# Attention and SiLU layers in one hand-ordered program: the last pair stored in whole rows, loads put behind other transposes, batches 2 to 4 in another order

## The chip, the core and the metric

The kernel runs on one core of one Trainium2 chip. The metric is the device time of one execution, in microseconds (us); three executions of the kernel before were timed, and a fourth was profiled.

## The reference

The computation is a Nyströmformer attention (8 batches, 8 heads, 576 tokens, head size 64, 32 landmarks), followed by two dense layers with a SiLU between them. Cut to what matters:

```
q_lm, k_lm = q, k as means over 18 neighbouring tokens        # 32 landmarks
A  = softmax(q  @ k_lm.T / 8)      # 576 x 32
Bm = softmax(q_lm @ k_lm.T / 8)    # 32 x 32
C  = softmax(q_lm @ k.T / 8)       # 32 x 576
Z  = Bm.T / (norm1 * norminf);  6 times: Z = 2 Z - Z @ Bm @ Z
x  = A @ Z @ C @ v                 # heads side by side: 4608 x 512
h  = x @ w_in;  out = (h * sigmoid(h)) @ w_out    # 512 -> 2048 -> 512
```

## The kernel before

The program is one long list of named steps, the string `SEQUENCE`. Each step emits its instructions on one engine, and each engine runs its own instructions in the order of the list. Nothing re-orders them on the chip: an engine waits for the first instruction in its queue, however much could be done behind it. A word is `name.batch` or `name@priority`; `/ACT`, `/DVE` or `/SP` picks the engine of a step that may run on several; `x<y` adds a wait of DMA x for the landing of DMA y; `*3` stands for three small matmuls that only fill time on TensorE.

The steps of batch b, by their names:

- `ld100.b` to `ld111.b`, `ld000.b` to `ld011.b`, `ldv0.b` to `ldv2.b` load k, q and v. They are issued by GpSimd (lines 401 and 418), which queues them in the order of the list. `ld1.b`, `ld0.b` do this for batch 2.
- `xt11.b`, `xt10.b`, `xt01.b`, `xt00.b` (line 551, batches 3 to 7) are DMA transposes of k and q, `ct0.b` and `ct1.b` (line 825, batches 2 to 7) DMA transposes of exp(C). `os...` are the stores of the output (line 988). SyncE issues all of these in the order of the list; only stores of the last pairs may also be issued by ScalarE.
- `lra`, `lrb`, `lrc`, `lrd` with `1.b` or `0.b` add up landmarks on VectorE, out of what `xt1..` and `xt0..` bring. `ltr`, `lmT`, `sb`, `pb`, `pbs`, `bmx`, `csb`, `f0` and others make Bm; `ns..`, `nsd..`, `fb..` are the six iterations for Z.
- `A.b`, `C.b` are the scores, `Ax..`, `Cx..` their exponentials on ScalarE, `etn..` the normalized A. `cv.b` multiplies exp(C) with v: it reads `ct0.b`, `ct1.b` and all of v. `wc.b`, `zbd.b`, `zt.b`, `ztc.b` make Z @ C @ v, and `m0.b` to `m3.b` multiply that with w_in; `mc..` are the copies of their results on VectorE or ScalarE.
- `h0.b` to `h15.b` finish the first layer, `g..` are its SiLUs on ScalarE (`hx`, `gx`: the last 64 columns of four batches in one tile).

The second layer works on pairs of 128-token tiles with seven products instead of eight (Strassen's scheme; `layer2_pair`). A pair has a number: `5000 + 100 b + 20 p` for batch b, half p, and 5340 or 5740 for the `gx` tile of four batches. `ss..` are its operand sums on VectorE, `p1` to `p7` its products on TensorE, 8 matmuls of 256 columns each. `c1`, `u2`, `c5`, `c21` copy results to the output tiles, `c11`, `c12`, `c22` add to them on VectorE. A pair has two output tiles: the low one is complete after `c11` (left half of its columns) and `c12` (right half), the high one after `c22` and `c21`. A store `os0` to `os3` sends 32 rows of 512 columns. `os@5100.0` is the low tile of pair 5100, in four stores, `os@5101.0` its high tile.

All TensorE steps share eight PSUM banks, and `SEQUENCE` decides which bank a step gets. The order of the DMAs is set by SyncE's and GpSimd's queues and by the `<` waits, which keep the transposes and the loads of one stage apart.

Of the kernel before, what the change touches and what calls it, by code (L numbers as in the profile page):

```python
# [42 lines left out]
trc15.2/DVE h14.0 g14.0 ns50.1 nsd50.1 zbd.1 ldv2.1 cv0.1 wc.1 tr114.2 trc114.2/DVE tr19.2
trc19.2/DVE zt.1 g8.0 ztc.1/ACT tr10.2 trc10.2/DVE lra1.2 h7.0 g7.0 m3.1 mc31.1/ACT mc30.1/ACT
m1.1 mc11.1/DVE mc10.1/ACT h1.0 g1.0 ld0.2 tr00.2 lrb1.2 tr09.2 tr014.2 trc014.2/DVE tr05.2
trc05.2/DVE trc09.2/DVE lrc1.2 trc00.2/ACT h12.1 g12.1 h7.1 g7.1 h15.1 m2.1 mc20.1/ACT m0.1
mc00.1/ACT mc21.1/ACT mc01.1/ACT wo0 o0@5001.0 h14.1 g14.1 g15.1 o0@5000.0 fold lrd1.2 lra0.2
lrb0.2 lrc0.2 lrd0.2 h11.1 g11.1 ltr0.2 ltr1.2 lmT1.2/DVE lmT0.2/ACT ss00@5020.0 ss10@5020.0
ss20@5020.0 ss30@5020.0 wo1 h5.1 o1@5000.0 sb.2 pb.2 pbs.2 pbr.2 bmx.2 bmt.2 wo2 wt00 bbd.2 h8.1
h3.1 o1@5001.0 o2@5000.0 wo3 o2@5001.0 wt01 g8.1 csb.2 o3@5001.0 oc@5001.0/ACT g3.1 g5.1 n1.2  # L50
nrm.2 stz.2 o3@5000.0 hx8.1 f0.2 gx8.1 h0.1 g0.1 oc@5000.0/ACT h2.1 h10.1 g10.1 h4.1 h1.1 g2.1
g1.1 wt11 wt21 stf0.2 fb00.2 ns00.2 h13.1 g13.1 wt31 nsd00.2 fb10.2 wt10 wt20 wt30 p1@5020.0
c1@5020.0/ACT ns10.2 nsd10.2 fb20.2 h9.1 h6.1 g4.1 g9.1 g6.1 ss00@5100.0 p5@5020.0 c5@5020.0/DVE
hx0.1 gx0.1 ss10@5100.0 l1done.0 C.2 Cx00.2 Cx10.2 p6@5020.0 u2@5020.0/DVE ld100.3 ld101.3 ld110.3
# [24 lines left out]
ld010.5 ld011.5 ss10@5200.0 lra1.4 lrb1.4 lrc1.4 ss10@5220.0 ss20@5220.0 lrd1.4 lra0.4 lrb0.4
os@5020.0 ss20@5200.0 l1done.2 ltr1.4 h1.3 h0.3 g0.3 g1.3 g12.3 h15.3 gx0.3 c1@5200.0/DVE  # L80
p6@5200.0 u2@5200.0/ACT os@5021.0 ss30@5200.0 c5@5200.0/DVE p3@5200.0 ss30@5220.0 lmT1.4/DVE
lrc0.4 lrd0.4 ltr0.4 lmT0.4/ACT g15.3 p1@5220.0 sb.4 pb.4 c1@5220.0/ACT xt11.5<ldv1.5
xt10.5<ldv1.5 c12@5200.0 p7@5200.0 c22@5200.0 p2@5200.0 c11@5200.0 p4@5200.0 c21@5200.0/ACT
p6@5220.0 xt01.5<ldv1.5 pbs.4 u2@5220.0/ACT pbr.4 l1done.3 bmx.4 bmt.4 bbd.4 ss00@5300.0
xt00.5<ldv1.5 C.4 lra1.5 csb.4 os@5120.0 Cx10.4 os@5121.0 Cx00.4 f0.4 p5@5220.0 Cx11.4 p7@5220.0
n1.4 lrb1.5 lrc1.5 os@5200.0 Cx01.4 nrm.4 ct0.4<ldv1.5 lrd1.5 c5@5220.0/ACT stf0.4 A.4 Ax00.4
Ax01.4 p5@5300.0 ltr1.5 fb00.4 Ax10.4 p3@5220.0 S10.4 Ln10.4 Ax11.4 wrc.4 stz.4 p1@5300.0 ns00.4
ss10@5300.0 ss20@5300.0 ss30@5300.0 c1@5300.0/ACT S00.4 S11.4 c22@5220.0 lra0.5 p4@5220.0 Ln11.4
Rs1.4 p6@5300.0 nsd00.4 lrb0.5 lrc0.5 lrd0.5 S01.4 fb10.4 lmT1.5/DVE ld000.6<xt00.5 ltr0.5
# [13 lines left out]
ct1.5<ldv1.6 u2@5340.0/ACT g5.4 g7.4 fb40.5 ns40.5 nsd40.5 fb50.5 p7@5340.0 ss30@5340.0 ns50.5
nsd50.5 c22@5340.0 h14.4 h12.4 g4.4 zbd.5 m0.4 g9.4 ldv2.5<xt00.4 g12.4 mc00.4/ACT mc01.4/DVE
cv0.5 wc.5 h11.4 h1.4 g11.4 g14.4 c11@5340.0 xt00.6<ldv1.6 zt.5 p3@5340.0 ztc.5/DVE etn0.5 g1.4
ldv0.7<xt00.6 c12@5340.0 ldv1.7<xt00.6 m0.5 ldv2.7<xt00.6 ld100.7<xt00.6 ld101.7 mc01.5/ACT m3.5
mc00.5/ACT ld110.7 ld111.7 m1.5 ldv2.6<xt00.5 mc10.5/ACT xt10.6<ldv1.6 l1done.6 xt11.6<ldv1.6
ldv0.6<xt00.5 ld000.7<xt00.6 mc11.5/DVE h0.4 h10.4 mc30.5/DVE h13.4 ld001.7 g10.4 g13.4 h4.5
# [1064 lines left out]
```

## Time and profile before

| | us |
|---|---|
| Median of three executions (240.06 to 241.44) | 240.55 |
| The profiled execution | 240.4 |
| Its span, first to last instruction | 238.7 |
| TensorE busy in the span | 230.6 |
| VectorE busy | 182.8 |
| ScalarE busy | 182.6 |
| GpSimd busy | 49.4 |

The profiled execution took 1.7 us more than its span. All instants in this text count from the span's start. The granted TensorE clock is 0.997 over the span. TensorE's matmuls overlap in the records, so that "busy" doesn't mean "at its peak"; what a step costs TensorE is the distance from its start to the start of the next one. Likewise the cost of an instruction in a queue of VectorE or ScalarE is the distance between two starts, a little under the duration in the record.

### The profile page before, as it was taken

The numbers are of one execution on the slowest core, as the hardware profiler recorded it, in microseconds if no ns is written. First come the engines' busy times: TensorE is split into PE (matmuls) and PEld (weight loads), VectorE is DVE, ScalarE is ACT, GpSimd is POOL, SyncE is SP. The second block draws the span as 40 slices with busy tenths as digits, with TensorE's granted clock in tenths as the row PEclk, the third lists the DMA queues.
The fourth block names the chain that finished last, engine by engine and source line by source line (L and its number), as shares of the span: only waits on it lengthen the run. The fifth ranks groups of instructions, "written<-read, shape, count | busy, mean of one in ns | idle before, by whom it ended". The sixth has DMA issues, their size and how long they took to land.

```text
span 238.7 us, 7507 instructions
## 1 busy us (share of the span) xinstructions
PE 230.6 (97%) x2948; PEld 163.7 (69%) x2948; DVE 182.8 (77%) x507; ACT 182.6 (76%) x434; POOL 49.4 (21%) x89
## 2 busy tenths in 40 slices
PE   6999999999999989999999999999999999999991
PEld 4887556456876745687878655768876645799881
DVE  2689889898998669939999789858998665538751
ACT  3599999989889988996867998999779797803100
POOL 0836652240055008103060074000000000000000
PEclk9999999999999999999999999999999999999998
DMA  6999999999999997998979999995527540012355
GB/s 251 265 202 186 202 212 205 208 205 180 160 162 190 231 229 137 202 155 174 196 132 202 174 163 243 220 173 119 104 54 112 122 102 1 3 44 48 89 124 142
DMA packets 56163, 37.72 MB, mean 158 GB/s; under 512 B 37056, under 2 KB 47552, under 8 KB 56128
## 3 DMA queue, kind: packets, MB, share of 16 engines
q0 software_dynamic: 15168, 17.18, 44.9%
q1 hardware_dynamic: 40144, 19.12, 39.0%
...
q8 instruction: 23, 0.38, 0.7%
...
## 4 chain that ended last, share of the span: by engine, by line
PE 90%; ACT 3%; DMA 3%; issue 1%; SPq 1%; DVE 0%; DVEq 0%
PE ps L337 87%; DMA gm<-in_q_dram 3%; PE ps L527 2%; ACT gm L923 1%; PE ps L813 1%; ACT L1126 1%; SPq L382 1%; ACT gx L946 0%; ACT pb L652 0%; ACT qk L347 0%; ACT et L753 0%; DVE wsb L856 0%; DVE ost L349 0%; ACT ost L347 0%; DVEq L856 0%
## 5 line engine op out<-in xcount | busy, mean ns | idle before, releaser
L923 ACT ACTIVATE gm<-ps 128x512 f16<-128x512 f32 x128 | 68.2, 626 | 4.9 <-PE ps L337 4.6
L337 PE MATMUL ps<-etn,m 128*128 128x64 bf16 (+1 forms) x512 | 70.9, 286 | 0.0
L337 PEld LDWEIGHTS <-gm 128*128 128x128 f16 x512 | 48.8, 98 | 11.0 <-issue 1.0
L337 PE MATMUL ps<-w_out_sb,gm 128*128 128x256 f16 (+1 forms) x392 | 52.5, 281 | 0.0
L337 PEld LDWEIGHTS <-m 128*128 128x128 bf16 x512 | 31.4, 98 | 23.0 <-issue 2.6
L337 PEld LDWEIGHTS <-ss 128*128 128x128 f16 x408 | 38.4, 98 | 7.8 <-issue 1.8
L337 PE MATMUL ps<-wt,ss 128*128 128x256 f16 x272 | 35.0, 273 | 0.0
L347 ACT COPY ost<-ps 128x256 f32<-128x256 f32 (+1 forms) x46 | 17.7, 392 | 18.8 <-PE ps L337 11.9
L1046 DVE TENSOR_TENSOR ost<-ost,ps 128x256 f32<-128x256 f32 x51 | 20.7, 415 | 10.7 <-PE ps L337 7.2
L349 DVE CAST m<-ps 128x512 bf16<-128x512 f32 x29 | 18.8, 685 | 3.6 <-PE ps L337 3.5
L418 POOL DMA_DIRECT2D v<-in_v_dram x24 | 14.5, 619 | 29.6 <-PE ps L337 27.3
L347 ACT CAST m<-ps 128x512 bf16<-128x512 f32 x35 | 18.9, 608 | 2.1 <-PE ps L337 2.1
L721 DVE SCALAR_TENSOR_TENSOR st<-st,ps 128x128 bf16<-128x128 bf16 (+2 forms) x54 | 13.6, 257 | 7.9 <-PE ps L337 7.1
L337 PE MATMUL ps<-w_out_sb,ss 128*128 128x256 f16 x136 | 17.6, 273 | 0.0
L401 POOL DMA_DIRECT2D qk<-in_k_dram x20 | 10.5, 546 | 34.1 <-DMA qT<-qk 15.8
L349 DVE COPY ost<-ps 128x256 f32<-128x256 f32 x24 | 10.1, 420 | 7.5 <-PE ps L337 7.1
L337 PE MATMUL ps<-wt,gm 128*128 128x256 f16 x120 | 15.5, 273 | 0.0
L946 ACT ACTIVATE gx<-ps 128x512 f16<-128x512 f32 x16 | 9.8, 619 | 7.5 <-PE ps L337 7.4
L696 DVE TENSOR_TENSOR fb<-st,hmask 128x256 bf16<-128x256 bf16 (+1 forms) x54 | 14.5, 273 | 1.1
L401 POOL DMA_DIRECT2D qk<-in_q_dram x20 | 10.5, 543 | 22.2 <-issue 14.0
L798 ACT ACTIVATE ce<-ps 128x288 bf16<-128x288 f32 x32 | 12.9, 417 | 2.3 <-PE ps L337 2.3
L763 ACT ACTIVATE ln<-ps 128x288 f32<-128x288 f32 x32 | 12.3, 428 | 3.0 <-PE ps L337 2.8
...
## 6 DMA issues: line engine op xcount, KB each, us to landing
out_dram<-ost SPq DMA_DIRECT2D x128, 64.0 KB, 2.9
...
```

Of the source, the lines that this page charges most:

```text
L337: nc.tensor.matmul(out=out_ap, lhsT=lhsT, rhs=rhs, start=start, stop=stop, skip_group_check=True)
L347: nc.scalar.copy(out=out, in_=in_)
L349: nc.vector.tensor_copy(out=out, in_=in_)
L401: lambda e, t=t, g=g, h=h, src=src: nc.gpsimd.dma_start(out=qk_r[b % 2][64 * h:64 * h + 64, t, g].rearrange("p j d -> p (j d)"), in_=src[b ...
L418: lambda e, a=a: nc.gpsimd.dma_start(out=v_r[b % 2][a * L:(a + 1) * L, :, :], in_=v[b].rearrange("h (l a x) d -> a l h (x d)", l=L, a=VA)[ ...
L696: nc.vector.tensor_tensor(out=fb[it % 2][:, g0:g1], in0=bc(sr[it % 3][:, g0:g1, 0:L], 4, 2), in1=bc(hmask, n, 1), op=OP.mult), [o], 14.5 + ...
L721: nc.vector.scalar_tensor_tensor(out=s2[:, g0:g1, lo:SW], in0=s[:, g0:g1, lo:SW], scalar=2.0, in1=ps[:, 0:NG * SW].rearrange("p (g x) -> p ...
L763: lambda e, g=g, c=c, ln=ln: nc.scalar.activation(out=ln[:, c], in_=bank(me["S", g, c])[:, 0:HS], func=AF.Ln),
L798: nc.scalar.activation(out=ce[:, :, 0:VP].rearrange("p (i c) (a l) -> p c a i l", c=2, a=VA)[:, c], in_=bank(me["C"], 2 * g + c)[:, 0:HS]. ...
L923: lambda e, dc=dc, cell=cell: nc.scalar.activation(out=gm[:, dc, :], in_=bank(cell["o"]), func=AF.Silu),
L946: lambda e, d0=d0, cell=cell, c=c: nc.scalar.activation(out=gx[:, d0:d0 + 8, c:c + 64], in_=bank(cell["o"]).rearrange("p (c x) -> p c x", ...
L1046: nc.vector.tensor_tensor(out=out_, in0=x, in1=y, op=OP.add)
```

## The change

There are three parts.

**Stores of the last pair.** The pair 5740 ends the kernel. Its low tile was stored in eight half rows (`os00` to `os03` after `c11`, `os10` to `os13` after `c12`, each 32 rows of 256 columns); it is now stored in four whole rows after both. The stores of the last four half-pairs were handed to SyncE and ScalarE one by one; they now stand directly behind the add that releases them, in turns by the two queues. The copy `c21@5720` moves from ScalarE to VectorE.

**Loads of batches 4 to 6.** `ld100.4` waited for `xt00.3` and now waits for `ct0.2`. In batch 6, the three v loads and four k loads are re-ordered: `ldv0.5` and `ldv2.5` lead and wait for `ct1.4`; `ldv1.6`, which comes last, keeps its wait for `xt00.5`. `ct0.5` and `ct1.5` no longer wait for `ldv1.6`.

**Order.** The steps from the end of batch 1's attention to the middle of batch 4's are listed in another order (from about 26 us to 142 us of the span), and some copies change between ScalarE and VectorE. No arithmetic is added or dropped; both lists hold 64 filler matmuls and the ScalarE program holds 12 table loads in each. GpSimd's queue keeps its order but for the two loads named; SyncE's queue keeps its order but for the last stores.

The diff, cut to what the text speaks of:

```diff
-mc10.0/DVE m0.0 f0.1 mc01.0/DVE mc00.0/ACT *1 ctm10.1 ctc10.1/DVE Rs1.1 csb.1 *1 h4.0 n1.1 m3.0
...
-ct0.2<ldv1.3 os@5000.0 ld100.4<xt00.3 ld101.4 ld110.4 ld111.4 lra1.3 fb30.2 ns30.2 p2@5020.0
...
-zbd.2 zt.2 ztc.2/ACT S10.3 Ln10.3 p4@5100.0 Cx11.3 ss00@5120.0 c11@5100.0 os@5100.0 ss10@5120.0
-ss20@5120.0 p1@5120.0 S01.3 Ln01.3 m3.2 mc31.2/ACT bmx.3 wrc.3 mc30.2/DVE c21@5100.0/ACT os@5101.0
-ct1.3<ldv1.4 m2.2 mc21.2/DVE mc20.2/ACT bmt.3 p5@5120.0 S00.3 m0.2 m1.2 mc11.2/DVE csb.3 bbd.3
...
-ns50.3 nsd50.3 zbd.3 h11.2 g11.2 h13.2 h3.2 cv0.3 wc.3 g4.2 g13.2 g3.2 etn1.3 zt.3 ztc.3/DVE
-etn0.3 p3@5120.0 c12@5120.0 m3.3 mc30.3/ACT m0.3 mc01.3/DVE mc00.3/ACT m2.3 mc21.3/ACT m1.3
...
-p2@5220.0 u2@5300.0/ACT p7@5300.0 ss00@5320.0 Ln01.4 c12@5220.0 lmT0.5/DVE sb.5 c21@5220.0/ACT
...
-c5@5300.0/ACT p3@5300.0 c12@5300.0 c22@5300.0 C.5 Cx01.5 cv0.4 wc.4 ldv1.6<xt00.5 bmt.5 Cx11.5
...
+mc10.0/DVE m0.0 mc01.0/DVE mc00.0/ACT *1 Rs1.1 csb.1 n1.1 nrm.1 ld1.2 ldv2.1 *1 h5.0 m3.0 ld0.2
...
+nsd10.1 h9.0 h10.0 fb20.1 ns20.1 g12.0 h8.0 g9.0 hx8.0 nsd20.1 fb30.1 g10.0 gx8.0 ctm10.1 etn0.1
...
+fb50.2 ld100.4<ct0.2 ld101.4 lmT0.3/ACT ld110.4 c12@5100.0 ld111.4 Rs1.2 A.3 os@5001.0 cv0.2
...
+m0.2 m1.2 mc01.2/ACT c11@5100.0 mc11.2/DVE p6@5120.0 f0.3 csb.3 n1.3 nrm.3 stf0.3 mc10.2/DVE
+fb00.3 p2@5120.0 c11@5120.0 h12.2 os@5100.0 os@5101.0 c5@5120.0/ACT u2@5120.0/ACT ct1.3<ldv1.4
...
+etn0.3 g2.2 c21@5120.0/ACT cv0.3 ld100.5<xt10.4 nsd50.3 ld101.5 wc.3 g9.2 zbd.3 p3@5120.0 zt.3
...
+mc10.3/ACT ldv0.4 m3.3 mc31.3/DVE h6.2 h2.3 lra1.4 h3.3 h4.3 mc30.3/ACT g6.2 h1.3 h7.3 g2.3 lrb1.4
...
+ss30@5220.0 xt00.5<ldv1.5 ss30@5300.0 C.4 Cx00.4 os@5120.0 lra1.5 p4@5200.0 p6@5220.0 pb.4 pbs.4
...
+fb20.4 C.5 pbr.5 ld101.6 ld110.6 c1@5320.0/DVE cv0.4 wc.4 bmx.5 ld111.6 ldv1.6<xt00.5 Cx01.5
+os@5201.0 p7@5300.0 ns20.4 c11@5320.0 p6@5320.0 nsd20.4 fb30.4 bmt.5 c22@5300.0 Cx11.5 os@5221.0
...
+os0@5720.0/ACT os2@5720.0/SP os3@5720.0/ACT p5@5740.0 c21@5720.0/DVE os0@5721.0/SP os1@5721.0/ACT
+os3@5721.0/SP os2@5721.0/ACT p7@5740.0 c5@5740.0/DVE p3@5740.0 c22@5740.0 c12@5740.0 os0@5740.0/SP
+os1@5740.0/ACT os3@5740.0/SP os2@5740.0/ACT p4@5740.0 c21@5740.0/DVE os0@5741.0/SP os1@5741.0/ACT
+os2@5741.0/SP os3@5741.0/ACT l1done.4

         for i, t, h, dep in ((lo_i, lo_t, 0, [c11, c12]), (hi_i, hi_t, 1, [c21, c22])):
-            if spread == 2 and not h:
-                ost_st[i] = [A(f"os{u}{m}@{prio + h}", [("SP", 0.46), ("ACT", 0.46)],
-                               lambda e, m=m, t=t, u=u, h=h: store(e, t, places[h], m, slice(
-                                   HM * u, HM * u + HM)), [dep[u]], prio + 0.1 * u,
-                               dma=0.1, lag=1.5) for u in range(2) for m in range(4)]
-            elif spread:
+            if spread:
                 ost_st[i] = [A(f"os{m}@{prio + h}", [("SP", 0.66), ("ACT", 0.5)],
                                lambda e, m=m, t=t, h=h: store(e, t, places[h], m), dep, prio,
                                dma=0.16, lag=3.0) for m in range(4)]
...
-                5000.0 + 100 * b + 40, 1, 2 * (b == B - 1))
+                5000.0 + 100 * b + 40, 1, int(b == B - 1))
```

More of the change, by code (lines that the diff above doesn't have):

```diff
@@ L43 @@
[L43 to L54, printed above, removed]
@@ L79 @@
[L79 to L89, printed above, removed]
-p2@5220.0 u2@5300.0/ACT p7@5300.0 ss00@5320.0 Ln01.4 c12@5220.0 lmT0.5/DVE sb.5 c21@5220.0/ACT
@@ L103 @@
[L103 to L108, printed above, removed]
@@ L115 @@
-c5@5400.0/DVE pb.6 u2@5400.0/DVE A.6 Ax00.6 Ax11.6 p3@5400.0 h3.5 Ax01.6 pbs.6 pbr.6 bmx.6 csb.6
-p1@5420.0 Ax10.6 h13.5 n1.6 g13.5 os@5321.0 c1@5420.0/DVE h10.5 nrm.6 g10.5 p7@5400.0 h9.5
-c12@5400.0 stz.6 bmt.6 bbd.6 S01.6 g3.5 S10.6 c22@5400.0 g1.5 f0.6 stf0.6 fb00.6 h6.5 h0.5 ns00.6
-p6@5420.0 g9.5 xt00.7<ldv1.7 nsd00.6 fb10.6 ns10.6 g0.5 g6.5 u2@5420.0/ACT S00.6 nsd10.6 p5@5420.0
-fb20.6 Ln10.6 ns20.6 p7@5420.0 c5@5420.0/ACT ss00@5500.0 xt10.7<ldv1.7 ss20@5500.0 S11.6 nsd20.6
-Ln01.6 ss10@5500.0 Ln11.6 xt01.7<ldv1.7 xt11.7<ldv1.7 fb30.6 os@5341.0 p4@5400.0 Ln00.6 Rs0.6
@@ L121 @@
-c22@5420.0 c21@5400.0/ACT lra1.7 lrb1.7 lrc1.7 lrd1.7 lra0.7 lrb0.7 lrc0.7 os@5340.0 lrd0.7 C.6
-Cx00.6 Cx11.6 Cx01.6 Cx10.6 wrc.6 p1@5500.0 Rs1.6 c1@5500.0/ACT p3@5420.0 c12@5420.0 p2@5500.0
-p2@5420.0 ltr1.7 ns30.6 lmT1.7/ACT c11@5500.0 ct1.6<ldv1.7 ltr0.7 p4@5420.0 lmT0.7/ACT sb.7
-p6@5500.0 nsd30.6 fb40.6 c11@5420.0 pb.7 c21@5420.0/ACT etn0.6 ss00@5520.0 ns40.6 etn1.6 A.7 pbs.7
-u2@5500.0/ACT Ax01.7 Ax10.7 p5@5500.0 p7@5500.0 Ax00.7 S10.7 S01.7 c5@5500.0/ACT S00.7
-ct0.6<ldv1.7 nsd40.6 Ln10.7 p2@5400.0 ss30@5500.0 fb50.6 ns50.6 pbr.7 bmx.7 Ln00.7 bmt.7 Ln01.7
@@ L127 @@
-csb.7 nsd50.6 n1.7 zbd.6 os@5401.0 Ax11.7 bbd.7 c11@5400.0 cv0.6 wc.6 c22@5500.0 C.7 nrm.7
-p3@5500.0 Cx01.7 zt.6 f0.7 Cx11.7 ztc.6/ACT Cx10.7 ss20@5520.0 stf0.7 p4@5500.0 Cx00.7 c12@5500.0
-S11.7 Ln11.7 ss10@5520.0 m1.6 os@5400.0 m0.6 m2.6 mc20.6/ACT mc21.6/ACT mc11.6/ACT mc10.6/DVE
-mc00.6/DVE p1@5520.0 wrc.7 stz.7 fb00.7 p2@5520.0 ns00.7 mc01.6/ACT nsd00.7 p5@5520.0 fb10.7
-c1@5520.0/ACT ns10.7 Rs0.7 ct0.7 c11@5520.0 p6@5520.0 c5@5520.0/ACT nsd10.7 fb20.7 ns20.7
-c21@5500.0/DVE h0.6 h5.6 h7.6 nsd20.7 h10.6 Rs1.7 g5.6 h3.6 ct1.7 etn1.7 fb30.7 ns30.7 g7.6
@@ new lines @@
+Ax00.3 wc.2 nsd50.2 Ax11.3 S01.3 ld010.4 ld011.4 pbs.3 c22@5100.0 Ax10.3 C.3 zbd.2 S00.3 p4@5100.0
+pbr.3 bmx.3 bmt.3 Ln01.3 zt.2 Cx11.3 S11.3 Cx01.3 Cx00.3 p1@5120.0 Ln11.3 ss00@5120.0 ss20@5120.0
+ztc.2/ACT ldv0.3 c21@5100.0/DVE ss10@5120.0 ldv2.3 Cx10.3 c1@5120.0/DVE Ln00.3 ldv2.4<xt00.3 m2.2
+mc21.2/DVE mc20.2/ACT m3.2 bbd.3 l1done.1 S10.3 Ln10.3 mc31.2/ACT mc30.2/DVE wrc.3 Rs0.3 p5@5120.0
+m0.2 m1.2 mc01.2/ACT c11@5100.0 mc11.2/DVE p6@5120.0 f0.3 csb.3 n1.3 nrm.3 stf0.3 mc10.2/DVE
+fb00.3 p2@5120.0 c11@5120.0 h12.2 os@5100.0 os@5101.0 c5@5120.0/ACT u2@5120.0/ACT ct1.3<ldv1.4
@@ new lines @@
+Ln00.5 l1done.7 ct0.5 ztc.4/ACT c1@5340.0/ACT c21@5320.0/ACT Rs0.5 ss10@5340.0 m3.4 mc30.4/ACT
+m1.4 mc31.4/DVE m2.4 mc21.4/ACT p6@5340.0 mc11.4/DVE ns20.5 mc20.4/ACT p2@5340.0 nsd20.5
+mc10.4/ACT h5.4 fb30.5 ns30.5 c5@5340.0/DVE nsd30.5 h7.4 h4.4 h9.4 ct1.5 u2@5340.0/ACT g5.4 g7.4
+fb40.5 ns40.5 nsd40.5 fb50.5 p7@5340.0 ss30@5340.0 ns50.5 nsd50.5 c22@5340.0 h14.4 h12.4 g4.4
+zbd.5 m0.4 g9.4 g12.4 mc00.4/ACT mc01.4/DVE cv0.5 wc.5 h11.4 h1.4 g11.4 g14.4 c11@5340.0
+xt00.6<ldv1.6 zt.5 p3@5340.0 ztc.5/DVE etn0.5 g1.4 ldv0.7<xt00.6 c12@5340.0 ldv1.7<xt00.6 m0.5
@@ new lines @@
+g8.5 p4@5340.0 h1.5 h5.5 g15.5 g12.5 gx8.5 lmT0.6/DVE sb.6 g14.5 g5.5 os@5300.0 hx8.4
+c21@5340.0/DVE ss00@5420.0 p1@5400.0 gx8.4 p5@5400.0 ss30@5400.0 c1@5400.0/ACT p6@5400.0 l1done.5
+ss20@5420.0 ss30@5420.0 ss10@5420.0 c5@5400.0/DVE pb.6 u2@5400.0/DVE A.6 Ax00.6 Ax11.6 p3@5400.0
+h3.5 Ax01.6 pbs.6 pbr.6 bmx.6 csb.6 p1@5420.0 Ax10.6 h13.5 n1.6 g13.5 os@5321.0 c1@5420.0/DVE
+h10.5 nrm.6 g10.5 p7@5400.0 h9.5 c12@5400.0 stz.6 bmt.6 bbd.6 S01.6 g3.5 S10.6 c22@5400.0 g1.5
+f0.6 stf0.6 fb00.6 h6.5 h0.5 ns00.6 p6@5420.0 g9.5 xt00.7<ldv1.7 nsd00.6 fb10.6 ns10.6 g0.5 g6.5
@@ new lines @@
+u2@5420.0/ACT S00.6 nsd10.6 p5@5420.0 fb20.6 Ln10.6 ns20.6 p7@5420.0 c5@5420.0/ACT ss00@5500.0
+xt10.7<ldv1.7 ss20@5500.0 S11.6 nsd20.6 Ln01.6 ss10@5500.0 Ln11.6 xt01.7<ldv1.7 xt11.7<ldv1.7
+fb30.6 os@5341.0 p4@5400.0 Ln00.6 Rs0.6 c22@5420.0 c21@5400.0/ACT lra1.7 lrb1.7 lrc1.7 lrd1.7
+lra0.7 lrb0.7 lrc0.7 os@5340.0 lrd0.7 C.6 Cx00.6 Cx11.6 Cx01.6 Cx10.6 wrc.6 p1@5500.0 Rs1.6
+c1@5500.0/ACT p3@5420.0 c12@5420.0 p2@5500.0 p2@5420.0 ltr1.7 ns30.6 lmT1.7/ACT c11@5500.0
+ct1.6<ldv1.7 ltr0.7 p4@5420.0 lmT0.7/ACT sb.7 p6@5500.0 nsd30.6 fb40.6 c11@5420.0 pb.7
@@ new lines @@
+c21@5420.0/ACT etn0.6 ss00@5520.0 ns40.6 etn1.6 A.7 pbs.7 u2@5500.0/ACT Ax01.7 Ax10.7 p5@5500.0
+p7@5500.0 Ax00.7 S10.7 S01.7 c5@5500.0/ACT S00.7 ct0.6<ldv1.7 nsd40.6 Ln10.7 p2@5400.0 ss30@5500.0
+fb50.6 ns50.6 pbr.7 bmx.7 Ln00.7 bmt.7 Ln01.7 csb.7 nsd50.6 n1.7 zbd.6 os@5401.0 Ax11.7 bbd.7
+c11@5400.0 cv0.6 wc.6 c22@5500.0 C.7 nrm.7 p3@5500.0 Cx01.7 zt.6 f0.7 Cx11.7 ztc.6/ACT Cx10.7
+ss20@5520.0 stf0.7 p4@5500.0 Cx00.7 c12@5500.0 S11.7 Ln11.7 ss10@5520.0 m1.6 os@5400.0 m0.6 m2.6
+mc20.6/ACT mc21.6/ACT mc11.6/ACT mc10.6/DVE mc00.6/DVE p1@5520.0 wrc.7 stz.7 fb00.7 p2@5520.0
```

136 lines of the change are left out of this document (74 added, 62 removed).

## The prediction

> **What bounds the kernel now.** I read the page's busy shares and chain first, then TensorE's timeline for its holes, then SyncE's timeline and waits for the DMAs that could make new ones, and last the end of the span.
>
> ```profile
> PE 230.6 (97%) x2948; PEld 163.7 (69%) x2948; DVE 182.8 (77%) x507; ACT 182.6 (76%) x434; POOL 49.4 (21%) x89
> PE 90%; ACT 3%; DMA 3%; issue 1%; SPq 1%; DVE 0%; DVEq 0%
> ```
>
> TensorE is the bound. The re-ordering adds and drops no matmul, so inside the span it can only take holes away or make new ones. Between 26 and 142 us, the re-ordered part, TensorE's timeline shows two holes worth a name:
>
> ```profile
> 27.62 0.28 PE L813 MATMUL ps<-idb,ce 128*128 128x128 bf16 x2 [0.48 <-issue]
> 86.69 0.56 PE L337 MATMUL ps<-v,ct 96*32 96x64 bf16 x48
> 87.90 0.29 PE L337 MATMUL ps<-zbd,wsb 128*128 128x128 bf16 x2 [0.66 <-DVE wsb L856]
> ```
>
> The first is inside `ctm10.1` (0.48 us); the second is `zt.3`, which follows `cv0.3` at once and waits for VectorE's `wc.3` (0.66 us). Together 1.1 us: that is all that the new order can win in its part. Everything else is cover that it can lose. The tightest cover is in SyncE's queue (start, us, what):
>
> ```profile
> 65.67 11.65 SPq L988 DMA_DIRECT2D out_dram<-ost  x16
> 78.61 2.54 SPq L825 DMA_TRANSPOSE ct<-ce  x2
> 81.26 6.96 SPq L551 DMA_TRANSPOSE qT<-qk  x4
> ...
> 100.91 6.85 SPq L551 DMA_TRANSPOSE qT<-qk  x4
> 107.85 7.37 SPq L988 DMA_DIRECT2D out_dram<-ost  x12
> 115.33 2.61 SPq L825 DMA_TRANSPOSE ct<-ce  x2
> ```
>
> ```profile
> SPq L551 <- DMA v<-in_v_dram: 7.6, 1, 7.6
> SPq L825 <- DMA out_dram<-ost: 1.2, 1, 1.2
> ```
>
> These rows are links of one chain. `ct1.3` (78.61) leaves when an earlier store has landed (the 1.2 us). Behind it go `ct0.3` and the four `xt..4`; the last, `xt10.4`, lands at 90.1 and releases GpSimd's loads of batch 5 (issued from 90.68). Their `ldv1.5` lands at 100.8 and releases `xt11.5` at 100.91 (the 7.6 us). From there SyncE works almost without a pause: four transposes, twelve stores, `ct0.4`, `ct1.4`. `ct1.4` lands at 119.94, and `cv0.4`, which reads it, starts at 120.64. The cover there is 0.7 us.
>
> **The order: what it wins.** `ctm10.1` moves away from `csb.1`, and `p3@5120.0` now stands between `cv0.3` and `zt.3`: its 0.87 us (the distance between products of 8 matmuls) covers `wc.3` and `zbd.3` (0.42 and 0.29 us). I count both holes as gone, 1.1 us; the first was waiting for nothing that the profile names, so between 0.66 and 1.1.
>
> **The order: what it costs.** Two things happen to the chain.
>
> *One product fewer ahead of `cv0.4`.* In the old list `p7@5300.0` ran before `cv0.4`, in the new one after it; all other TensorE steps ahead of it are the same. So TensorE comes to `cv0.4` earlier by 0.87 plus the holes won, at about 118.7, but `ct1.4` isn't there before 119.94. If the chain keeps its times, `cv0.4` starts at 119.99, 0.65 us sooner than before, with 0.87 us more behind it: the end is 0.22 us later. The 1.1 us are given back, whatever they were. In general the end moves by 0.22 plus the shift of the chain.
>
> *The chain starts later.* `os@5100.0` needs `c11@5100.0`, which VectorE did at 72.02 to 72.43 (store at 72.46). In the new order VectorE does it behind `mc21.2`, `bbd.3`, `mc30.2` and `wrc.3`. `mc21.2` needs `m2.2`, whose matmuls ran from 74.03 to 74.43; in the new list they come 0.23 earlier (0.35 of `S10.3` and `m3.2` gone from ahead, 0.12 of `S00.3` added), and with the first hole gone 0.7 earlier. From 73.7 to 74.2 on, VectorE's queue takes 0.60 + 0.20 + 0.60 + 0.25 and 0.42 for `c11` itself: `os@5100.0` at 75.8 to 76.3, take 76.05, which is 3.6 later. The eight stores of pair 5100 (0.47 from one to the next) are out at 79.8. But `ct1.3` also waits until the first of them has landed. These eight took 4.4 to 5.8 us from issue to landing, 5.1 on average, with loads in flight; those at 88 to 91 us took 2.6 to 3.2. So 76.05 + 0.31 + 5.1 = 81.5 for `ct1.3`, between 79.8 (SyncE alone) and 82.4 (5.8), against 78.61: 2.9 later (1.2 to 3.8). One part comes back: `xt00.4` took 2.61 us to issue, from 81.26 to 83.87, while loads were landing until 83.44; the next ones took 1.3. Starting at 84.1 it would be free of them, 1.3 us. The shift is then +1.6 (-0.1 to +2.5; the middle row is the same eight stores, so I take it), and nothing later in the chain absorbs it: GpSimd's loads start on `xt10.4`, SyncE's next transposes on those loads.
>
> The landing of `ct0.3` moves from 84.92 to about 86; `cv0.3` comes at about 85.9. A wait of some tenths there costs nothing more, since `cv0.4` waits for the same chain later. The same holds for VectorE, which stops twice because its queue is in order: `lra1.4` now stands right behind `mc31.3`, reached at about 89.5 and released by `xt10.4` at 91.7 (behind it `c1@5200.0`, not needed before 93); `lra1.5` now stands ahead of `pbs.4`, `bmx.4`, `c22@5220.0`, `n1.4`, and 5.2 us of VectorE lie between its start at 108.6 and what `S00.4` waits for. That puts `S00.4` 0.5 us later than before, less than `cv0.4` will be.
>
> **The loads.** `ld100.4` behind `ct0.2` leaves about 0.7 us later than its 65.43, and its group then pauses anyway until `cv0.2` releases `ldv1.4`: nothing. `ct0.5` without its wait could leave earlier than 127.34, and `cv0.5` wasn't late before: nothing, either way.
>
> **The last stores.** ScalarE's queue ends the span:
>
> ```profile
> 226.49 5.61 ACTq L988 DMA_DIRECT2D out_dram<-ost  x9
> 232.20 0.38 ACT L347 COPY ost<-ps 128x256 f32<-128x256 f32 x1 [6.67 <-DMA out_dram<-ost]
> 232.28 4.09 ACTq L988 DMA_DIRECT2D out_dram<-ost  x8
> 225.30 10.14 SPq L988 DMA_DIRECT2D out_dram<-ost  x12
> ```
>
> The last copy, `c21@5740`, ends at 234.32, but ScalarE issues its last store from 235.89 to 236.37 (landed 237.67, span end 238.69), SyncE its last until 235.44: ScalarE had to send half rows and `os2@5721` first, and `c21@5720` sat behind nine stores. The new list has four stores fewer, at 0.47 each, and alternates. `c12@5740` ends at 233.44: two stores on each queue until 234.31. Then `os@5741`, two on each: 234.41 to 234.80, 234.85 to 235.3. Landing 1.3 to 1.5 later as in the rows: 236.7, 1.0 us sooner. `c21@5720` on VectorE takes 0.42 of a queue that idles 0.45 before each of its adds: nothing.
>
> **Sum.** 238.69 + 0.22 + 1.6 - 1.0 = 239.5 of span, plus 1.7 around it 241.2; the profiled run (240.4) lies 0.15 below the median, so 241.3 against 240.55.
>
> **Rivals.** *The chain gets short* (faster; chance 0.2). If the first store lands in 3.2 us as those at 88 to 91 us did at most, `ct1.3` leaves at 79.8 and the shift is -0.1; and if SyncE's slow store at 111.23 (1.77 us instead of 0.43) goes too, it is -1.4. Then `cv0.4` finds `ct1.4` landed and TensorE keeps its 1.1 us: 240.55 - 1.1 - 1.0 = 238.4. It decides from a shift of -0.4 on. For it: the slow issues come while loads are in flight, and the loads move. Against: the stores still run beside batch 4's loads.
>
> *The slow transpose stays slow* (slower; 0.2). If the 2.61 us of `xt00.4` isn't due to the loads, the 1.3 us don't come back: shift 2.9, 242.6. For it: `xt10.6` took 2.4 us after the loads had landed. Against: `xt10.5` sped up just as the last load landed. The Trainium skill, "DMA: Bandwidth & Descriptors", section "Rules for kernel authors", says that a transpose next to ordinary DMAs needs nothing; read so, the loads would not be what slowed it, and by the rule the time is this 242.6. That is a rule about safety more than speed, and the rows so far lean the other way.
>
> *The end earns little* (0.1). If eight whole rows in two us land in 2.0 instead of 1.3, 0.3 remains of the 1.0: 242.0. The rows of the end go from 1.15 to 3.05 us. The Trainium skill, same page, section "Latency and other measured facts", puts the memory's part of a DMA's latency at 0.2 us, and 2 us at high load; by the latter the whole gain would be gone.
>
> **How the numbers follow.** The forecast's case has 0.5: its shift of -0.1 to 2.5 gives 239.6 to 242.2, and 0.15 of it lies over 0.5% slow. 0.5% is 1.2 us, about what a measurement of this kernel can tell from no change. Slower: 0.15 + 0.19 + 0.06 = 0.40; faster: 0.17 of the first rival and 0.02; the same: 0.41. The range takes in the first rival's time nearly and the second's with its bound: 238.5 to 243.0.
>
> **What would show it.** After: `os@5100.0` issued at about 76, `ct1.3` near 81.5, `xt10.4` landing past 91, a hole on TensorE ahead of `cv0.4` of 1.5 to 3 us, no hole at `zt.3`, last store out by 235.3 plus the shift. No hole at `cv0.4` would prove the chain wrong; another hole ahead of it, larger, would mean that I missed the bound.

## The result: 0.7% slower, and the profile after

The changed kernel takes 242.15 us (median of 12 executions, 241.13 to 243.35), the kernel before beside it 240.72 (239.78 to 244.47). The ratio is 1.0068, 95% interval 1.0039 to 1.0098, taken over the undisturbed (fast) executions alone, so it isn't the quotient of the two medians. The change made the kernel slower; 0.68% is above the 0.5% that the prediction set as its bound, but the interval reaches below it. The time is 0.85 us above the forecast of 241.3. The profiled execution of the changed kernel (241.13 us, span 239.4) is the fastest of its twelve, so a second profile of it is shown further down.

The page of the changed kernel, busy times and shares of the chain that ended last:

```profile
PE 231.3 (97%) x2948; PEld 163.3 (68%) x2948; DVE 181.8 (76%) x508; ACT 182.5 (76%) x433; POOL 49.5 (21%) x89
PE 83%; DMA 9%; ACT 5%; issue 1%; SPq 1%; DVE 0%
```

TensorE is still the bound. In the chain, DMA now has 9% instead of 3%. Where it comes in is seen on TensorE's timeline at `cv0.4` (start in us, duration, engine, line; in brackets the idle time before and what ended it):

```profile
119.36 0.44 PE L335 MATMUL ps<-qT,lmT 64*32 64x288 bf16 x16
120.26 0.36 PE L335 MATMUL ps<-v,ct 96*32 96x64 bf16 x24 [0.46 <-DMA ct<-ce]
121.03 0.36 PE L335 MATMUL ps<-v,ct 96*32 96x64 bf16 x24 [0.41 <-DMA ct<-ce]
121.32 1.05 PE L335 MATMUL ps<-w_out_sb,gm 128*128 128x256 f16 x8
```

`C.5` is followed by `cv0.4`, whose first 24 matmuls wait for `ct0.4` and whose last 24 for `ct1.4`; `p7@5300.0` comes only then. The two transposes end this chain in SyncE's queue:

```profile
64.70 16.49 SPq L986 DMA_DIRECT2D out_dram<-ost  x16
81.61 2.54 SPq L823 DMA_TRANSPOSE ct<-ce  x2
84.26 5.59 SPq L549 DMA_TRANSPOSE qT<-qk  x4
...
102.01 6.90 SPq L549 DMA_TRANSPOSE qT<-qk  x4
109.00 7.38 SPq L986 DMA_DIRECT2D out_dram<-ost  x12
116.48 2.58 SPq L823 DMA_TRANSPOSE ct<-ce  x2
```

The stores, 11.65 us in the kernel before, now stretch over 16.49 (the pause ahead of `os@5100.0` counts in it), and `ct1.3` leaves 3.0 us later. At `ct0.4` 1.15 us of that are left. TensorE's last matmul starts at 234.65 instead of 233.59. The hole at `zt.3` is gone; `cv0.3`, `p3@5120.0` and `zt.3` follow each other without a bracket:

```profile
86.77 0.56 PE L335 MATMUL ps<-v,ct 96*32 96x64 bf16 x48
87.26 1.05 PE L335 MATMUL ps<-w_out_sb,ss 128*128 128x256 f16 x8
88.19 0.28 PE L335 MATMUL ps<-zbd,wsb 128*128 128x128 bf16 x2
```

### The profile page after: what moved, and what is told of

It reads as the page before. It is cut to its first block, busy times and chain, and to the rows that moved or that the text cites. A ratio compares the mean times of both kernels' runs of the same rounds, so it can differ in the third digit from the quotient of the medians.

```text
span 239.4 us, 7488 instructions
## 1 busy us (share of the span) xinstructions
PE 231.3 (97%) x2948; PEld 163.3 (68%) x2948; DVE 181.8 (76%) x508; ACT 182.5 (76%) x433; POOL 49.5 (21%) x89
## 4 chain that ended last, share of the span: by engine, by line
PE 83%; DMA 9%; ACT 5%; issue 1%; SPq 1%; DVE 0%
PE ps L335 81%; DMA out_dram<-ost 5%; DMA gm<-in_q_dram 3%; PE ps L525 2%; DMA ct<-ce 1%; ACT ln L765 1%; ACT L1119 1%; ACT ln L761 0%; ACT m L345 0%; PE ps L811 0%; ACT L921 0%; ACT pb L650 0%; SPq L380 0%; ACT qk L345 0%; ACT et L751 0%
## 5 line engine op out<-in xcount | busy, mean ns | idle before, releaser
L335 PE MATMUL ps<-etn,m 128*128 128x64 bf16 (+1 forms) x512 | 71.9, 286 | 0.4 <-DVE m L347 0.2
L335 PE MATMUL ps<-w_out_sb,gm 128*128 128x256 f16 (+1 forms) x392 | 53.1, 281 | 0.0
L345 ACT COPY ost<-ps 128x256 f32<-128x256 f32 (+1 forms) x43 | 16.5, 393 | 12.2 <-PE ps L335 11.7
L347 DVE CAST m<-ps 128x512 bf16<-128x512 f32 x30 | 19.4, 685 | 4.0 <-PE ps L335 3.9
L347 DVE COPY ost<-ps 128x256 f32<-128x256 f32 x27 | 11.4, 421 | 7.0 <-PE ps L335 6.6
```

Source lines behind the costliest of these rows:

```text
L335: nc.tensor.matmul(out=out_ap, lhsT=lhsT, rhs=rhs, start=start, stop=stop, skip_group_check=True)
L345: nc.scalar.copy(out=out, in_=in_)
L347: nc.vector.tensor_copy(out=out, in_=in_)
```

## The experiments

Each kernel was timed against the kernel before on the same chip, in three groups (e1 to e4; a1, e6, f1, f2; b2, e5, f3, f4). This table has what their verdicts rest on. The first 20 us of a profile scatter by 1.6 us from run to run, so the instants in it are counted from a matmul of `S01.1`, at 23 to 25 us of the span. `A.5` is the point behind which TensorE's order is the same in all kernels. "os@5100.0 issued" is the start of the last of its four stores (the first starts 1.3 to 1.8 us earlier, 2.4 in f2). The wait is the sum of the brackets at `cv0.4`; the tail goes from the start of the last matmul to the last landing.

| kernel | ratio to before (95%) | os@5100.0 issued | ct1.4 landed | wait at cv0.4 | A.5 starts | tail |
|---|---|---|---|---|---|---|
| before | | 50.5 | 96.2 | none | 98.4 | 4.08 |
| b2: before again | 0.9978 (0.9937 to 1.0020) | 50.3 | 96.4 | none | 98.3 | 3.44 |
| changed | 1.0068 (1.0039 to 1.0098) | 54.9 | 97.4 | 0.87 | 99.6 | 3.54 |
| a1: changed again | 1.0109 (1.0057 to 1.0161) | 54.9 | 98.5 | 1.69 | 101.7 | 3.51 |
| e1: stores behind xt10.4 | 1.0027 (1.0003 to 1.0050) | 65.0 | 96.0 | none | 98.5 | 3.53 |
| e2: cv0.4 behind p7 | 1.0073 (1.0035 to 1.0110) | 54.9 | 97.7 | none | 99.1 | 3.53 |
| e3: old order, new end | 1.0020 (0.9990 to 1.0051) | 51.4 | 98.5 | 0.15 | 99.9 | 3.73 |
| e4: new order, old end | 1.0071 (1.0042 to 1.0099) | 54.9 | 98.0 | 1.19 | 100.3 | 3.29 |
| e6: changed, old gates | 1.0086 (1.0048 to 1.0125) | 54.9 | 98.0 | 1.29 | 100.2 | 3.63 |
| e5: late store alone | 1.0046 (1.0012 to 1.0079) | 54.8 | 97.7 | none | 99.2 | 3.43 |
| f1: hole at zt.3 filled | 0.9969 (0.9947 to 0.9990) | 50.4 | 95.9 | none | 98.0 | 3.46 |
| f2: f1, stores behind xt10.4 | 1.0032 (1.0000 to 1.0065) | 66.8 | 96.4 | none | 97.9 | |
| f3: f1 with the new end | 1.0017 (0.9990 to 1.0044) | 50.2 | 96.2 | none | 97.9 | 3.58 |
| f4: f1, h2.2 moved up | 0.9994 (0.9963 to 1.0026) | 50.4 | 95.7 | none | 98.2 | 3.40 |

b2 says how far a ratio goes astray: the kernel before against itself comes out at 0.9978. Single ratios are good to between 0.2 and 0.5%, as their intervals say; instants in the profiles say more. From the start of `A.5` to the start of the last matmul all profiles but three take 111.4 to 111.5 us (a1 112.0, e2 111.9, f2 118.2), so what the new order costs is to be found ahead of `A.5`. There, where `cv0.4` waits in the new order, `A.5` moves by what the landing of `ct1.4` moves: against the first profile of the kernel before, 1.20 and 1.18 us in the changed kernel, 1.83 and 1.81 in e4, 1.80 and 1.77 in e6. Only a1 loses more, as is shown below.

### The stores out of the way (e1)

```diff
-fb00.3 p2@5120.0 c11@5120.0 h12.2 os@5100.0 os@5101.0 c5@5120.0/ACT
+fb00.3 p2@5120.0 c11@5120.0 h12.2 c5@5120.0/ACT
...
-ns50.3 xt10.4<ldv1.4 etn0.3
+ns50.3 xt10.4<ldv1.4 os@5100.0 os@5101.0 etn0.3
```

> The changed kernel, with one thing moved in its order: the two steps of SyncE that issue the stores of the pair before (os@5100.0, os@5101.0) stand behind the transposed load xt10.4 instead of ahead of the transposed loads of exp(C). Theory 1 (the late store holds SyncE, and cv0.4 waits for ct0.4 and ct1.4 at the end of that chain): ct1.3 no longer waits behind the stores and is issued at 77 or before (81.61 in the changed kernel), xt10.4 is issued at 84 to 86 (88.45), the holes of 0.53 and 0.57 us at and inside cv0.4 are gone, the last matmul of the closing product starts about 1.0 us earlier (233.6 instead of 234.65), and the time is 0.8 to 1.2 us below the changed kernel's. Rival A (the loss lies in the small holes of the new order of VectorE and ScalarE between 26 and 54 us): the hole at cv0.4 may go, but the same time comes up as idle time elsewhere, and the time stays within 0.3 us of the changed kernel's. Rival B (the gates of the loads of batches 5 and 6 set ct0.4, not the stores): ct0.4 lands at 120.2 as before, and nothing is won.

SyncE's timeline and TensorE's at `cv0.4` in e1:

```profile
75.22 3.67 SPq L822 DMA_TRANSPOSE ct<-ce  x2
79.05 8.64 SPq L548 DMA_TRANSPOSE qT<-qk  x4
87.78 6.78 SPq L985 DMA_DIRECT2D out_dram<-ost  x11
...
120.34 0.55 PE L334 MATMUL ps<-v,ct 96*32 96x64 bf16 x48
```

`ct1.3` leaves over 6 us earlier than in the changed kernel, `ct1.4` lands at 96.0 instead of 97.4, and all 48 matmuls of `cv0.4` run without a bracket. `A.5` starts at 98.5, where the kernel before has it. The ratio falls from 1.0068 to 1.0027, some 1.0 us (the two intervals touch, but `A.5` says the same, 1.2 us). Theory 1 holds in place and size: the late stores in front of the transposes make the wait.

### The product back in front (e2)

```diff
-ld110.6 c1@5320.0/DVE cv0.4 wc.4 bmx.5 ld111.6 ldv1.6<xt00.5 Cx01.5 os@5201.0 p7@5300.0 ns20.4
+ld110.6 c1@5320.0/DVE bmx.5 ld111.6 Cx01.5 os@5201.0 p7@5300.0 cv0.4 wc.4 ldv1.6<xt00.5 ns20.4
```

> The changed kernel, with cv0.4 (and wc.4 and the load that overwrites its input) put back behind the product p7@5300.0, the order that the kernel before has there. Nothing is changed on SyncE up to ct1.4. Theory 1: p7@5300.0 covers 0.87 us of the wait for ct1.4, so of the 1.1 us of holes at and inside cv0.4 some 0.2 are left; ct1.4 still lands near 121.0; the last matmul of the closing product starts 0.8 to 0.9 us earlier than in the changed kernel, and the time is 0.7 to 0.9 us lower. Rival A (holes of the new order spread over the start): no more than 0.3 us is won. Rival B (cv0.4 later makes its readers, wc.4 and the products of the next pair, wait): the 0.87 comes back as a hole behind cv0.4 and the time is that of the changed kernel.

No wait is left at `cv0.4`, yet the ratio is 1.0073: nothing is won. VectorE's and TensorE's timelines in e2 show what is late instead:

```profile
123.05 0.42 DVE L853 TENSOR_TENSOR wsb<-ps,pbs 128x256 bf16<-128x256 f32 x1 [0.50 <-PE ps L334]
...
126.77 0.23 PE L334 MATMUL ps<-st,fb 128*128 128x64 bf16 x2 [0.15 <-DVE fb L693]
```

The first line is `wc.4`, which waits for `cv0.4`; `nsd20.4`, the next link of the iterations for Z, stands behind it in VectorE's queue. TensorE then waits for it, at `p7@5320.0` (0.16) and at `ns40.4` (0.32, of which the bracket shows 0.15). Both lie behind `A.5`, which is 0.5 us earlier than in the changed kernel: the 0.5 is won there and given back. Rival B holds: what waits for `ct1.4` isn't `cv0.4` alone but, through `wc.4`, the queue of VectorE. Another 0.37 and 0.21 lie inside `A.4` and ahead of `p4@5220.0`, where VectorE was held at `lra1.5` until `xt10.5` landed. So the place of `p7@5300.0` isn't worth the 0.87 us that theory 1 gave it.

### The two halves apart (e3, e4)

e3 takes the list of the kernel before up to `c21@5700.0` and the code and list of the changed kernel from there; e4 is the reverse.

> The kernel before in its order up to the last pair's last eviction, with the end of the changed kernel alone (whole rows, stores by two queues in turn). Theory 1 (the end earns about 0.5, since its last stores land 1.7 to 2.0 us after they are issued instead of 1.3): the last landing is 3.5 us behind the start of the last matmul (4.085 in the kernel before), TensorE's end is that of the kernel before, and the time is 0.4 to 0.7 us below the kernel before's. By the prediction's own sum the end alone would earn 1.0. Rival (the end earns nothing, all that is seen in one profile is scatter): within 0.2 us of the kernel before.

> The changed kernel's order up to the last pair's last eviction, with the end of the kernel before. Theory 1: TensorE's end is that of the changed kernel (last matmul about 1.07 us later than in the kernel before, holes of about 1.1 us at and inside cv0.4), the tail is that of the kernel before (4.1 us), and the time is 1.0 to 1.3 us above the kernel before's and 0.4 to 0.7 above the changed kernel's. Rival (the new end is what costs, not the order): the time is within 0.3 us of the kernel before's.

e4 keeps the whole loss (1.0071, 1.19 us of wait at `cv0.4`), so the order costs, as theory 1 has it. But it isn't 0.4 to 0.7 above the changed kernel, and e3 isn't below the kernel before: the new end earns nothing. e3's profile can't be used for the order, since a wait of 0.96 us ahead of `ltr0.3`, on VectorE's sums, put its chain late; no other profile has that.

### The changed kernel again, and its loads (a1, e6)

> The changed kernel itself once more, beside the three kernels that follow. Theory 1 (late stores hold SyncE until cv0.4 waits): again a hole of 0.4 to 0.7 us at cv0.4 and one inside it, and 0.5 to 1.0% above the kernel before. Rival (the holes at cv0.4 were one profile's accident): no such hole, and the loss must lie in holes that every profile shows, those ahead of h5.0, h13.0, h1.1 and m1.1. Of the end: theory E1 (the new end earns 0.5) expects the last landing 3.5 us behind the start of the last matmul.

The holes are there again, and larger. TensorE's timeline in a1, and below it windows of a few us (after the width come busy time and number of instructions for PE, PEld, DVE, ACT and POOL, then the granted clock, the DMA share and GB/s):

```profile
121.88 0.36 PE L335 MATMUL ps<-v,ct 96*32 96x64 bf16 x24 [1.41 <-DMA ct<-ce]
122.51 0.36 PE L335 MATMUL ps<-v,ct 96*32 96x64 bf16 x24 [0.28 <-DMA ct<-ce]
...
123.92 1.89 PE L335 MATMUL ps<-wt,ss 128*128 128x256 f16 x8
```

```profile
122.00:124.00 2.00, 1.72 (x59) 1.40 (x52) 0.89 (x3) 1.33 (x6) 0.95 (x2) 0.89 0.75 169
124.00:126.00 2.00, 2.00 (x27) 1.08 (x23) 1.82 (x6) 0.15 (x1) 2.00 (x5) 0.50 0.98 139
126.00:127.00 1.00, 1.00 (x20) 0.46 (x5) 0.62 (x2) 0.72 (x3) 0.96 (x2) 0.51 1.16 174
```

`ct1.4` lands 1.1 us later than in the first profile, and TensorE waits 1.69 instead of 0.87. Of the 1.1 us, 0.6 come from the twelve stores ahead of `ct0.4`, which took 7.96 us in SyncE's queue instead of 7.38, and 0.3 from the landing of `ct1.4` itself. Behind the wait its clock falls to 0.50: `p6@5320.0` takes 1.89 us where 8 such matmuls take 1.04, and by 127 us some 1.5 us more are gone. This run took 244.16 us, the slowest of its six.

e6 is the changed kernel with the old gates:

```diff
-ld100.4<ct0.2
+ld100.4<xt00.3
...
-ldv0.5<ct1.4 ldv2.5 ld100.6 ld101.6 ld110.6 ld111.6
 ldv1.6<xt00.5 os@5201.0 os@5221.0 os@5220.0
-ct0.5 ct1.5
+ld100.6<xt00.5 ld101.6 ld110.6 ld111.6 ct0.5<ldv1.6 ldv0.5<xt00.4 ct1.5<ldv1.6 ldv2.5<xt00.4
```

> The changed kernel with the gates and places of its loads as in the kernel before: ld100.4 behind xt00.3 instead of ct0.2, the loads of batch 6 and the later ones of batch 5 behind xt00.5 and xt00.4 at their old places in the order, ct0.5 and ct1.5 with their waits. Stores and compute stay as changed. Theory 1 (the loads move neither os@5100.0 nor ct1.4): time within 0.3 us of the changed kernel, holes at cv0.4 as there. Rival (the loads, gated elsewhere, compete with the transposes of batch 4 or 5): ct1.4 lands 0.5 us or more earlier, and the time falls by 0.4 or more.

Same holes, same `os@5100.0`, 1.0086: the gates neither cost nor earn, within the 0.4% that can be told.

### The late store in the old order (e5)

```diff
-ss00@5120.0 c11@5100.0 os@5100.0 ss10@5120.0
+ss00@5120.0 ss10@5120.0
...
-c21@5100.0/ACT os@5101.0 ct1.3<ldv1.4 m2.2
+c21@5100.0/ACT m2.2
...
-m1.2 mc11.2/DVE csb.3
+m1.2 mc11.2/DVE c11@5100.0 os@5100.0 os@5101.0 ct1.3<ldv1.4 csb.3
```

> The kernel before with one thing of the new order alone: c11@5100.0 stands on VectorE behind mc11.2, so that the stores os@5100.0 are issued some 3 us later; SyncE keeps its order (stores, ct1.3, ct0.3, transposed loads). Product p7@5300.0 stays ahead of cv0.4. Theory 1: counted from the first product of S01.1, os@5100.0 is issued at 53 to 55 us (50.4 before, 54.9 in the changed kernel), xt10.4 lands 1.5 to 3 us later than before, ct1.4 lands 0.5 to 1.3 later, at 96.7 to 97.5; cv0.4, due at 96.9 in this order, waits 0 to 0.6 us for it, and the time is 0 to 0.6 us above the kernel before's (with the product in front of it less than in the changed kernel). Rival (in the old order the chain has room): ct1.4 lands as before, no hole at cv0.4, same time.

SyncE's timeline in e5, and a line of TensorE's:

```profile
65.80 16.25 SPq L986 DMA_DIRECT2D out_dram<-ost  x16
82.49 2.54 SPq L823 DMA_TRANSPOSE ct<-ce  x2
85.14 5.68 SPq L549 DMA_TRANSPOSE qT<-qk  x4
...
77.14 0.19 PE L335 MATMUL ps<-bm,hmask 128*128 128x64 bf16 x1 [0.90 <-DVE m L347]
```

Moving one add on VectorE and the stores that need it (SyncE keeps its order) gives the SyncE queue of the changed kernel: 16.25 us of stores, and `ct1.4` at 97.7 instead of 96.2 to 96.4. So the late store alone makes the chain late in the old order too. The time of this kernel says less, because the edit also handed `csb.3` a PSUM bank that VectorE frees late (0.90 us, the last line), and behind that hole TensorE reaches `cv0.4` just as `ct1.4` lands.

### One hole filled by itself (f1, f2, f4)

f1, on the list of the kernel before:

```diff
-zbd.3 h11.2 g11.2 h13.2 h3.2 cv0.3 wc.3 g4.2 g13.2 g3.2 etn1.3 zt.3 ztc.3/DVE etn0.3 p3@5120.0 c12@5120.0 m3.3
+zbd.3 etn1.3 etn0.3 h11.2 g11.2 h13.2 h3.2 cv0.3 wc.3 g4.2 g13.2 g3.2 p3@5120.0 zt.3 ztc.3/DVE c12@5120.0 hx8.2 m3.3
...
-m1.3 mc20.3/ACT h2.2 hx8.2 g2.2
+m1.3 mc20.3/ACT h2.2 g2.2
```

> The kernel before with one hole of TensorE filled and nothing else of the change: p3@5120.0 ahead of zt.3, hx8.2 ahead of m3.3, and etn1.3 and etn0.3 on VectorE ahead of wc.3, where it idles 1.3 us. Stores, loads and end stay as before. Theory 2 (a hole filled where the order around it stays is won in full; the changed kernel lost its gain to new small holes and to the late stores): the holes of 0.66 us ahead of zt.3 and of 0.3 ahead of h2.2 are gone, TensorE's last matmul comes 0.8 to 1.0 us earlier counted from the first product of S01.1, and the time is 0.5 to 0.9 us below the kernel before's. Rival (what is won at zt.3 is waited for at the next landing, cv0.4 behind ct1.4, where the kernel before has 0.7 us to spare): a hole of 0.2 us or more at cv0.4, and no more than 0.5 us is won.

TensorE's timeline in f1:

```profile
86.76 1.05 PE L335 MATMUL ps<-w_out_sb,ss 128*128 128x256 f16 x8
87.64 0.28 PE L335 MATMUL ps<-zbd,wsb 128*128 128x128 bf16 x2
87.76 0.63 PE L335 MATMUL ps<-etn,m 128*128 128x64 bf16 x16
88.50 1.51 PE L335 MATMUL ps<-w_in_sb,zt 64*32 64x512 bf16 x32
```

The hole at `zt.3` is gone, but 0.28 us come up ahead of `m3.3`, and the one ahead of `h2.2` grows from 0.36 to 0.65 (both over the usual distance between such matmuls; too short for a bracket). That banks are now freed in another order would explain it, but isn't shown. `A.5` starts 0.3 to 0.4 us earlier than in the two profiles of the kernel before, half of what was expected; the ratio, 0.9969, is in the range given, though it lies only 0.1% under that of b2, the kernel before itself. No wait comes up at `cv0.4`, so the rival falls.

> The same as the kernel f1 beside it, and the stores os@5100.0 and os@5101.0 moved on SyncE behind xt10.4, as in the first experiment. Theory 2: ct1.3 is issued at 75 to 76 (78.6 in the kernel before), the chain of transposes up to ct1.4 is 0.5 to 1.5 us early and cv0.4 has that much more to spare; the time is that of f1 or up to 0.4 us lower, and it scatters less from run to run. Rival (the stores, put off to 88 to 93 us, now share the DMA with the loads of batch 5 and make those late): xt00.5 lands later than in f1 and the time is 0.3 us or more above it.

The rival's two signs are there: 1.0032, and `xt00.5` lands 0.8 us later. `ct1.3` leaves 3 us earlier than in f1 but lands no earlier (60.8 against 60.6), while the loads of batch 4 are still landing; the stores then run beside the loads of batch 5, and `ldv1.5` lands at 78.8 instead of 77.4. Moving the stores helps where they are late, and wins nothing where they aren't. Where the 0.6% over f1 is lost isn't shown: `A.5` starts at 97.9, no later than in f1, and no wait comes up at `cv0.4`. (Further on, at 149.74 us, TensorE had waited 4.06 us, because VectorE stood 4.3 us until a transposed load of batch 6 landed. No other profile has that, so only earlier instants are used.)

f4 moves `h2.2` ahead of `m3.3` as well:

> The kernel f1 with h2.2 as well moved up, behind hx8.2 and ahead of m3.3, since f1 still has a hole of 0.28 us ahead of m3.3 (it waits for ztc.3) and one of 0.65 ahead of h2.2 (its PSUM bank waits for mc01.3). Theory 2: both holes shrink by 0.4 us together or more, and the time is 0.2 to 0.6 us below f1's, 0.994 to 0.996 of the kernel before. Rival (ScalarE, which idles 0.77 us ahead of mc30.3, sets the stretch: a bank comes free no earlier): the hole moves to m1.3 and h6.2, and the time is that of f1.

The holes go to `m1.3` (0.44) and the step behind it (0.54), as the rival has it, and `A.5` gains nothing on f1. f4, which contains f1's edit, came out at 0.9994 in another group: f1 is the only version whose interval lies below 1, and its time wasn't reproduced. The instants hold better: with f1's edit `A.5` starts at 98.0, 97.9, 97.9 and 98.2 (f1 to f4), against 98.4 and 98.3 without.

### The end, settled (b2, f3)

> The kernel before itself, as one of the timed kernels: its ratio to its own other runs tells how far a ratio goes astray by chance, and its profile gives a second look at the end. Expected: a ratio of 1.000 within 0.003. Theory E0 (the new end earns nothing; the 4.1 us from the start of the last matmul to the last landing in the first profile was one draw): 3.3 to 3.7 us this time, no more than the 3.5 of the new end. Theory E1 (the new end earns 0.5): 3.9 to 4.2 us again.

> The kernel f1 (kernel before with the hole at zt.3 filled) with the end of the changed kernel. Theory E0: the last landing is 3.5 to 3.6 us behind the start of the last matmul, and the time is that of f1 within 0.3 us, that is 0.997 of the kernel before. Theory E1: 0.5 us below f1, 0.995 of the kernel before.

The tail of the kernel before is 3.44 us in b2. All old ends but the first have 3.29 to 3.46 (f2 left out), all new ones 3.51 to 3.73. In b2, ScalarE's queue at the end:

```profile
225.84 4.82 ACTq L988 DMA_DIRECT2D out_dram<-ost  x9
230.75 0.37 ACT L347 COPY ost<-ps 128x256 f32<-128x256 f32 x1 [5.87 <-DMA out_dram<-ost]
230.83 4.22 ACTq L988 DMA_DIRECT2D out_dram<-ost  x8
```

and both queues in the changed kernel:

```profile
227.56 8.78 ACTq L986 DMA_DIRECT2D out_dram<-ost  x12
224.95 11.31 SPq L986 DMA_DIRECT2D out_dram<-ost  x16
```

In b2 nine stores ahead of `c21@5720` took 4.82 us, in the first profile 5.61: there the copy came 1.39 us ahead of the last matmul's start, here 2.18. So the 4.08 was one draw: it goes with the row of stores that held this copy. The new end does issue its last store earlier, 1.68 us behind the last matmul's start (236.33) against 2.13 in b2. But its last four stores land 1.7 to 2.0 us after issue, 0.2 us apart, where the last four in b2 took 1.3 to 1.6. Once `c12@5740` is done the new list sends eight stores of 64 KB, the old one four of 64 and four of 32; the other half rows were under way before. Beyond that, from the last landing to the end of the span is 1.2 us in new ends and 0.9 to 1.0 in old ones, for a reason that the profile doesn't show. E0 holds, if anything with a small loss (f3 is 0.23% above f4 in the same group, less than their intervals can tell apart).

## Why the prediction was right or wrong

The sign and the mechanism were right, the size was short: a rise of 0.75 us was forecast (to 241.3), and the medians rose by 1.4 (to 242.15). The first profile of the changed kernel even has the span of the prediction's sum, 239.4 against 239.5, but by luck. Against the first profile of the kernel before, `A.5` came 1.2 us later where the sum had 1.8, the end earned 0.3 (0.5 of tail, less 0.2 behind the last landing) where it had 1.0, and 0.1 was won ahead of `S01.1`, where nothing was changed. The steps, one by one:

- **`os@5100.0` at 76.05: came at 77.18.** Two reasons. TensorE reached `m2.2` at 74.23, no earlier than before, so the gain at the first hole, which this step counted on, hadn't come. And VectorE wasn't free for `mc21.2`: the new list also hands it `c21@5100.0` and `c1@5120.0`, which ScalarE did before, and puts them ahead of it. The prediction left these two out. `m2.2` had ended at 74.64, but `mc21.2` (the second line of VectorE's timeline below) started at 75.09, directly behind `c1@5120.0` (the first). From there to `c11` VectorE took 1.66 us, as summed.

```profile
74.75 0.42 DVE L347 COPY ost<-ps 128x256 f32<-128x256 f32 x1
75.09 0.68 DVE L347 CAST m<-ps 128x512 bf16<-128x512 f32 x1
```

- **`ct1.3` at 81.5: came at 81.61, by two errors that cancel.** The stores left 1.13 us later than forecast, and the first of them landed in 4.04 us instead of 5.1. What `ct1.3` waited for was right: the row of eight stores was out at 81.19, that first store landed at 81.53, and `ct1.3` left 0.08 us behind. In the first profile of the kernel before, in b2, a1 and e5 it left 0.07 to 0.08 us behind this landing as well.
- **`xt00.4` back to 1.3 us: right** (1.30). The rival that it stays slow falls. In e1, where the transposes leave earlier, `xt00.4` took 3.11 us while loads were landing until 82.04, and `xt11.4`, issued 0.24 us behind the last of them, still 2.57. So slow issues come with the loads or right behind them; which of the transfers in flight holds them isn't shown. The Trainium skill, "DMA: Bandwidth & Descriptors", section "Rules for kernel authors", says that a transpose next to ordinary DMAs needs nothing. Read as a rule about time, that doesn't hold here.
- **"Nothing later in the chain absorbs it": wrong.** `xt10.4` landed 2.8 us late, `ct1.4` 1.04. From `ld100.5` to the landing of `ldv1.5` the first profile of before took 10.1 us, b2 8.9, the changed kernel 8.4.
- **Shift 1.6: right on average, which is 1.7.** Over the profiles with the late store (changed, a1, e2, e4, e5, e6), `ct1.4` lands at 97.4 to 98.5, without it (e3 left out) at 95.7 to 96.4.
- **The hole at `cv0.4`, 1.5 to 3 us: 0.87, 1.19, 1.29 and 1.69.** In place and kind right, but three of the four lie below the range. TensorE came to `cv0.4` at about 119.7 instead of 118.7, since the 1.1 us of holes weren't won.
- **"In general the end moves by 0.22 plus the shift": the 0.22 isn't there.** `A.5` moves by the shift alone. The prediction let all of `cv0.4` wait for `ct1.4`; its first 24 matmuls, about 0.25 us, wait only for `ct0.4` and run before.
- **1.1 us of holes to win: not there.** From `S01.1` to `A.5` TensorE has the same steps in the kernel before and in e1, the new order without the late store. The brackets in this stretch fall from 1.14 us (0.48 and 0.66, the two holes of the prediction) to the 0.24 of a new one ahead of `h5.0` (below). Yet `A.5` comes at 98.4 and 98.5. What the brackets lose comes back in gaps that are too short for a bracket.

```profile
27.82 0.61 PE L334 MATMUL ps<-etn,m 128*128 128x512 bf16 x2 [0.24 <-DVE m L346]
```

- **Loads: nothing. Right** (e6). **VectorE stopping at `lra1.5`: nothing. Nearly right**: up to 0.6 us in e2, where `xt10.5` lands late.
- **The last stores, 1.0 us sooner: the step that failed.** When the last store goes out was right: 1.68 us behind the start of the last matmul, against 1.71 in the sum. But the sum compared with one profile whose tail was 0.64 us longer than b2's, and it let the last stores land in 1.3 to 1.5 us, where the last four of eight whole rows took 1.7 to 2.0. That is the rival "the end earns little", which had a chance of 0.1 and gave 242.0. Without the 1.0, the prediction's own sum is 240.5 of span and 242.3 us; measured 242.15.

What stays open: why the twelve stores and the landing of `ct1.4` were slower in a1 than in the first profile of the same kernel, why e1, whose `A.5` is where the kernel before has it, still measures 0.27% above it, and why the span ends 0.2 us later behind the last landing with the new end.
